# A state-space layer and an MLP in one kernel: decay rows in one load, constants regrouped, and a new head of the written order

## The chip, the cores and the metric

The kernel runs on one core of one Trainium2 chip. The core has five engines with instruction lists of their own: TensorE (PE, matmuls; PEld is its weight load), VectorE (DVE), ScalarE (ACT), GpSimd (POOL) and SyncE (SP), which here only issues transfers. Sixteen DMA engines move data between HBM and the on-chip memory. The metric is the device time of one execution in microseconds, the median of several runs.

## The reference, cut to what matters

```python
# x (4, 8, 768, 32), a (4, 8, 768), B and C (4, 8, 768, 16), all float32
log_a = np.log(np.clip(a, 1e-06, 1.0))
for c in range(nc):                       # chunks of 32 along the sequence
    cum = np.cumsum(la, axis=-1)
    L = np.exp(cum[..., :, None] - cum[..., None, :]) * causal
    M = np.einsum('bhin,bhjn->bhij', Cc, Bc) * L
    y_intra = np.einsum('bhij,bhjd->bhid', M, xc)
    y_inter = np.einsum('bhin,bhnd->bhid', Cc, state) * np.exp(cum)[..., None]
    y[:, :, sl] = y_intra + y_inter
    state = decay_full * state + sum_j(B_j x_j * decay_from_j)
x = y.transpose(0, 2, 1, 3).reshape(3072, 256)
h = x @ w_in                              # (256, 2048)
g = 0.5 * h * (1 + tanh(c * (h + 0.044715 * h**3)))
out = g @ w_out                           # (2048, 256), result (3072, 256)
```

The first half is a linear recurrence with a decay `a` per head and position, computed by chunks; the second is a two-layer MLP with the tanh form of GELU on its result.

## The kernel before, in words

The sequence of each of the 4 batches is cut into 6 chunks of 128 positions (`Q`), so there are 24 chunks, taken in 12 pairs, called units `u`. All 8 heads of a chunk are worked on together. Decays are not handled as logarithms: a reversed scan along each chunk gives the product of decays from a position to the chunk's end (`R`), B is multiplied by it, C by its reciprocal, and then the score of two positions is a plain product with a causal mask. The steps of a unit:

- `mul`, `T` or `tw`, `E` or `ew`: multiply B and C by their decays, turn them on TensorE, copy the result out of PSUM. Batch 0 has forms of its own: chunks 0 to 3 come first (`load_bc0`, `mulb`, `mulc`, `tw`, `ew`), chunks 4 and 5 later (`load_bc1`, `mul1`, `T1`, `ce1`, `bh1`). Batches 2 and 3 are turned by DMA through HBM.
- `G`: scores of a unit into four PSUM banks, `ga` (two) and `gb` (two).
- `M.u.0` and `M.u.1`: VectorE multiplies `ga` and `gb` by the causal mask (line 605). For unit 0 the second half goes another way: `GE` (line 610), ScalarE copies the two `gb` banks, and `ME` (line 616), GpSimd masks the copies.
- `XX`, `XD`, `xn`: unpack x of chunks 0 to 3 with 0/1 matrices on TensorE, and the chunks' contribution to the state; `D` is that contribution elsewhere.
- `S` and `SP`: new state, and the state scaled by the chunk's decay and spread over a block mask (lines 676 and 683, VectorE).
- `Y` and `yev`: the output of the pair, and its copy to `xm`, the input of the MLP.
- `s1.u.i` (line 709): four matmuls of the first projection into one of two `hp` banks; `gelu.u.i` (line 713) takes it to `gT`; `s2.c.q` (line 727): four matmuls of the second projection of chunk `c`; `oev` copies out, `store` writes.

The weights come as float32 in four quarters each (`load_wi`, `load_wo`), and each quarter is cast in two halves (`wi.q.k`, `wo.q.k`, line 316 on GpSimd, 314 on ScalarE, 318 on VectorE).

The decays of chunks 0 to 3 of batch 0 have a chain of their own at the start: `load_aq` (line 159, four loads of 32 rows), `clipq` (328), `Rq` (331, the scan), `tpq` (342, a transpose), `peq` (351), `recip0` (348), then `mulb`, `mulc`. `load_a` brings all decays as two halves for `clip`, `R`, `tp2`, `tp6`.

Constants are built at the start: `c_ident`, `c_tri`, `c_bmask`, `c_m8` on GpSimd, `c_cz` (a zeroed tile for C, line 254) on GpSimd, `c_wz`, `c_zero`, `c_unp` (the 0/1 matrices, lines 227 and 258 to 261), `c_sel` (271 and 273), `c_m4` (277), `c_par` on VectorE, `c_warm` (loads ScalarE's GELU table).

The order is written out by hand in `ORDERED`: one list of step names, which fixes the order of each engine's instructions. A suffix names the engine (`:A` ScalarE, `:D` VectorE, `:P` GpSimd, `:S` SyncE), `~n` is n blocks of 128 columns of filler matmuls (line 697), which compute nothing that is used, and `+4` four such blocks in front of a step. The tile framework adds the waits between engines. `deps` and `takes` are kept for the tool that made the list and do not act here.

Of the kernel before, what the change touches and what calls it, by code (L numbers as in the profile page):

```python
# [87 lines left out]
def kernel(  # L88
# [164 lines left out]
    def c_cz():  # L253
        nc.gpsimd.memset(cz, 0.0)
# [708 lines left out]
```

## Time and profile before

| | us |
|---|---|
| median of 3 runs (lowest, highest) | 116.99 (116.8, 117.34) |
| span of the profiled execution, first to last instruction | 115.1 |
| PE busy | 109.4 (95%) |
| ACT busy | 75.1 (65%) |
| DVE busy | 68.7 (60%) |
| POOL busy | 15.1 (13%) |
| share of DMA time of the 16 engines on the main queue | 53.9% |

The profile shows one execution: its instructions by engine with start and length, what an engine waited for, and the chain of work that ended last. The profiled execution itself is given by its span; the timed runs contain some 1.9 us more, which lies around the first and the last instruction. Rows of instructions read: start, length, engine, line, operation, out<-in, form, count, and in brackets the idle time before and what ended it. The granted clock is 1.00 all through on this core.

### The profile page before, as it was taken

What the parts mean: (1) busy time and instruction counts of PE and PEld (TensorE: products, weight loads), DVE (VectorE), ACT (ScalarE), POOL (GpSimd) and SP (SyncE); (2) the same over time, 40 slices, a digit from 0 to 9 for tenths busy, and PEclk for the clock granted to TensorE, in tenths of its full rate; (3) what the DMA queues carried; (4) which work ended last, traced back from release to release, by engine and by line L of the source; (5) the groups of instructions that cost most, each with busy time, mean ns of one, the idle gap of its engine ahead of it and who ended that gap; (6) DMA issues with size and microseconds to landing.
All of it is one profiled execution on the core that took longest, in us unless ns stands there. A gap on an engine that the chain in (4) does not pass through costs nothing.

```text
span 115.1 us, 3372 instructions
## 1 busy us (share of the span) xinstructions
PE 109.4 (95%) x1425; PEld 92.2 (80%) x1425; DVE 68.7 (60%) x135; ACT 75.1 (65%) x149; POOL 15.1 (13%) x32
## 2 busy tenths in 40 slices
PE   6999799999999999999999999999999999999990
PEld 2354578978877979799898998998989989999970
DVE  6688799998799989196966281546827421000100
ACT  3119889978657767657576486377766765685710
POOL 6564274122220000020002000000000000000000
PEclk9999999999999999999999999999999999999999
DMA  2999999949969828959478760000014014001132
GB/s 65 236 280 286 397 293 311 278 84 218 225 109 226 214 64 203 192 147 265 102 158 184 174 178 0 6 0 0 0 50 138 0 49 139 0 0 51 46 103 79
DMA packets 43006, 15.97 MB, mean 139 GB/s; under 512 B 36656, under 2 KB 41456, under 8 KB 42992
## 3 DMA queue, kind: packets, MB, share of 16 engines
q1 hardware_dynamic: 42848, 15.68, 53.9%
q8 instruction: 11, 0.18, 0.6%
q10 hardware_dynamic: 144, 0.08, 0.4%
q14 instruction: 3, 0.02, 0.1%
HBM read 11.04 MB, written 3.93 MB: 130 GB/s over the span
## 4 chain that ended last, share of the span: by engine, by line
PE 82%; DMA 8%; SPq 4%; POOL 1%; issue 1%; ACT 0%
PE hp L709 36%; PE o_ps L727 33%; DMA wf<-in_moe_w_out_dram 8%; PE yb L727 3%; PE ga L595 3%; PE yb L650 2%; PE yb L659 2%; SPq L190 1%; PE hp L628 1%; SPq L162 1%; SPq L159 1%; SPq L150 1%; POOL w_out_sb L316 1%; POOL w_in_sb L316 1%; SPq L183 1%
## 5 line engine op out<-in xcount | busy, mean ns | idle before, releaser
L713 ACT ACTIVATE gT<-hp 128x512 bf16<-128x512 f32 x96 | 53.3, 595 | 24.5 <-PE hp L709 24.0
L709 PE MATMUL hp<-xm,w_in_sb 128*128 128x256 bf16 x384 | 51.9, 273 | 0.5 <-ACT pend L314 0.3
L727 PE MATMUL o_ps<-w_out_sb,gT 128*128 128x256 bf16 x352 | 46.4, 273 | 0.0
L709 PEld LDWEIGHTS <-w_in_sb 128*128 128x128 bf16 x384 | 41.2, 114 | 3.2 <-issue 1.7
L727 PEld LDWEIGHTS <-gT 128*128 128x128 bf16 x384 | 37.0, 98 | 4.7 <-issue 0.8
L318 DVE COPY o_sb<-o_ps 128x256 f32<-128x256 f32 x7 | 3.0, 424 | 22.4 <-PE o_ps L727 18.4
L605 DVE TENSOR_TENSOR m<-ga,tri 128x1024 bf16<-128x1024 f32 x12 | 14.6, 1216 | 0.0
L605 DVE TENSOR_TENSOR m<-gb,tri 128x1024 bf16<-128x1024 f32 x11 | 13.4, 1219 | 0.5 <-PE gb L595 0.5
L697 PE MATMUL yb<-wz 128*128 128x512 bf16 (+2 forms) x24 | 8.2, 491 | 1.1 <-DVE warm L222 1.1
L314 ACT ACTIVATE o_sb<-o_ps 128x256 f32<-128x256 f32 x15 | 5.6, 382 | 4.1 <-PE o_ps L727 3.0
L683 DVE SCALAR_TENSOR_TENSOR sp_new<-s_new,pend,bmask 128x256 bf16<-128x256 f32 x17 | 8.0, 479 | 0.1
L316 POOL CAST x<-x_t 128x512 bf16<-128x512 f32 x5 | 3.2, 648 | 34.9 <-DMA x_t<-in_x_dram 22.9
L676 DVE SCALAR_TENSOR_TENSOR s_new<-s_new,pend,hp 128x64 f32<-128x64 f32 x13 | 3.6, 279 | 5.7 <-PE hp L628 5.5
L697 PEld LDWEIGHTS <-wz 128*128 128x128 bf16 x25 | 2.9, 126 | 5.0 <-issue 3.6
L659 PE MATMUL yb<-m,x 128*32 128x128 bf16 x192 | 6.1, 219 | 0.0
L650 PE MATMUL yb<-ce,sp_new 128*32 128x128 bf16 x160 | 5.3, 220 | 0.0
L595 PE MATMUL ga<-ce,bh 32*128 32x256 bf16 x48 | 4.7, 272 | 0.1
L314 ACT ACTIVATE xm<-yb 128x512 bf16<-128x512 f32 x8 | 4.8, 597 | 0.0
L595 PE MATMUL gb<-ce,bh 32*128 32x256 bf16 x48 | 4.7, 273 | 0.0
L727 PE MATMUL yb<-w_out_sb,gT 128*128 128x256 bf16 x32 | 4.1, 273 | 0.0
L659 PEld LDWEIGHTS <-x 128*32 128x32 bf16 x192 | 3.8, 97 | 0.4 <-issue 0.2
L650 PEld LDWEIGHTS <-sp_new 128*32 128x32 bf16 x160 | 3.0, 96 | 1.0 <-issue 1.0
(108 smaller groups left out, 78.4 us busy)
## 6 DMA issues: line engine op xcount, KB each, us to landing
out_dram<-o_sb SPq DMA_DIRECT2D x24, 128.0 KB, 2.0
x_t<-in_x_dram SPq DMA_DIRECT2D x20, 128.0 KB, 3.8
wf<-in_moe_w_in_dram SPq DMA_DIRECT2D x4, 512.0 KB, 8.3
wf<-in_moe_w_out_dram SPq DMA_DIRECT2D x4, 512.0 KB, 8.9
bc_t<-in_B_dram SPq DMA_DIRECT2D x3, 384.0 KB, 4.8
bc_t<-in_C_dram SPq DMA_DIRECT2D x3, 384.0 KB, 4.3
scr<-bc SPq DMA_DIRECT2D x4, 192.0 KB, 3.1
x_t<-in_x_dram SPq DMA_DIRECT2D x1, 512.0 KB, 4.8
```

The source lines that it names most:

```text
L314: nc.scalar.activation(o, i, AF.Copy)
L316: nc.gpsimd.tensor_copy(out=o, in_=i)
L595: nc.tensor.matmul(out=gbank(g)[:, 256 * k:256 * k + 256], lhsT=bh_of(2 * u + k)[gs], rhs=ce_of(2 * u + k)[gs], start=True, stop=True, til ...
L605: nc.vector.tensor_tensor(out=m_of(u)[:, 2 * i:2 * i + 2].rearrange("p g k e t -> p (g k e) t"), in0=gx[i].rearrange("p g (k t) -> p (g k) ...
L650: nc.tensor.matmul(out=y4[32 * j:32 * j + 32, k, w], lhsT=sp[:, 32 * h:32 * h + 32], rhs=ce_of(gc)[:, h % 2], start=first(j), stop=False, ...
L659: nc.tensor.matmul(out=y4[32 * j:32 * j + 32, k, w], lhsT=X16[u][:, k, 32 * h:32 * h + 32], rhs=m[:, h // 2, h % 2, :], start=first(j), st ...
L676: nc.vector.scalar_tensor_tensor(out=s_new, in0=state[("s", gc - 1)], scalar=pend_of(gc), in1=d, op0=ALU.mult, op1=ALU.add)
L683: nc.vector.scalar_tensor_tensor(out=sp_new.rearrange("p (g d) -> p g d", g=4), in0=(XN[0][:, H * D:H * D + 64] if gc == 0 else state[("s" ...
L697: nc.tensor.matmul(out=t[:, 0:m * 128], lhsT=wz, rhs=w3.to_broadcast([128, m, 128]), start=True, stop=True, skip_group_check=True)
L709: nc.tensor.matmul(out=hp[:, j * T:(j + 1) * T], lhsT=w_in_k[:, w, q, k], rhs=xm[:, w, u * T:(u + 1) * T], start=(w == 0), stop=(w == 1))
L713: nc.scalar.activation(gts[u][:, 2 * i:2 * i + 2], hps.pop((u, i)).rearrange("p (j t) -> p j t", j=2), AF.Gelu_apprx_tanh)
L727: nc.tensor.matmul(out=ops[gc], lhsT=gts[u][:, fi, k * Q:(k + 1) * Q], rhs=w_out_sb[:, fi, :], start=(fi == 0 and (u > 0 or k == 0)), stop ...
```

## The change

- `load_aq` becomes one load of 128 rows on SyncE, the first in its list; row 8 i + h holds positions from 32 i on of head h of batch 0. Only each fourth group of eight rows is used as a chunk. B's and C's loads follow, C first, then x of chunks 0 to 3, then weights; `load_a` goes to SyncE and stands behind two weight loads.
- `c_unp`'s zeroing becomes a step `c_unp0` on GpSimd, and its four copies one copy with a diagonal pattern. `c_cz` goes to ScalarE, as a copy of the zeroed `wz`. `c_m4`, `c_sel` and `c_unp` move behind the start of the decay chain on VectorE. `mulb` goes from GpSimd to VectorE, `mulc.1` from VectorE to GpSimd.
- `GE` and `ME` are used for units 0 and 1 instead of unit 0 alone (`GEU`), and `M.1.1` is gone.
- `SP` gets a form for GpSimd (two instructions), used for chunks 3, 6, 7 and 8.
- The list is new from its start to `castx.7` (unit 4); from there on only engine suffixes on `SP` are added. Unit 1's first projections are put between those of unit 0. The filler is 48, 4, 8 and 3 blocks instead of 53, 9, 8, 2, 13 and 4.

```diff
+GEU = (0, 1)
 ORDERED = """
-c_wz c_ident c_zero c_unp load_aq.2:A load_bc0.1 c_tri load_aq.1:S load_aq.3:S load_aq.0:A c_m8
-c_sel c_warm c_m4 load_bc0.0 load_x4 clipq Rq tpq load_a.0:A load_a.1:S peq ~53 ppq pendq:A
-load_wi.0 c_cz c_bmask recip0 mulc.0:D mulc.1:D mulb:P ~9 tw.1 tw.0 ew.0.0:D c_par ew.0.1:A tw.2
-ew.0.2:A x4.1:D ~8 G.0 clip ew.1.0:A ew.1.1:A load_wi.1 M.0.0 GE.3 x4.0:P GE.2 load_wi.2 ~2 XX.0
-XD.0 load_wo.0 xn.0:A ew.1.2:A SP.0 S.0.0 xn.1:A wi.0.0:A wi.0.1:A R ~13 G.1 S.0.1 load_wi.3 XX.1
-load_bc1.0 xn.2:A ME.3:P ME.2:P pe Y.0 XD.1 pp yev.0.0.2:A S.1.0 load_wo.1 load_bc1.1 SP.1 S.1.1
-load_wo.2 wi.1.1:P M.1.0 wi.2.0:P wo.0.0:D pend:A wo.0.1:P wi.2.1:P SP.2 wi.1.0:A M.1.1 s1.0.0
...
+c_wz load_aq c_ident c_unp0:P c_zero clipq load_bc0.1 load_bc0.0 Rq tpq c_m4 recip0 peq c_cz:A
+c_warm mulc.0:D c_sel mulb:D c_bmask c_tri c_unp mulc.1:P ~48 tw.2 tw.1 ~4 tw.0 ew.1.0:D ew.1.2:D
+ew.1.1:A ew.0.2:A ew.0.1:A load_x4 ew.0.0:A ~8 G.0 ppq M.0.0 pendq:D x4.1:P load_wi.0 load_wi.1
+load_a.1:S load_a.0:S load_wo.0 x4.0:A GE.0.2 XX.0 GE.0.3 xn.0:A xn.1:A load_wi.2 load_bc1.0
+load_bc1.1 load_wo.1 ME.0.2:P XD.0 G.1 ME.0.3:P GE.1.2 GE.1.3 S.0.0 SP.0 ~3 Y.0 XX.1 XD.1 S.0.1
+M.1.0 SP.1:D wi.1.1:D S.1.0 c_par ME.1.3:D SP.2:D clip S.1.1 wo.0.1:D wo.0.0:D R yev.0.0.2:A xn.2:A
+wi.1.0:A wi.0.1:P wi.0.0:P ME.1.2:P wi.2.1:P c_m8 wo.1.0:P s1.0.0 gelu.0.0 xn.3:A load_wi.3 s1.0.1
+gelu.0.1 load_wo.2 s1.0.2 Y.1 s1.0.3 gelu.0.2 yev.1.0.2:A gelu.0.3 load_bc.1.0 load_wo.3 load_bc.1.1
+load_x.2 s1.1.0 gelu.1.0 load_x.3 s1.1.1 gelu.1.1 wi.3.0:P wi.3.1:P wo.2.1:P wi.2.0:D tp2 recip1
+s2.0.0.0.o mul1.1 mul1.0 wo.1.1:D s1.0.4 gelu.0.4 s1.1.2 s2.0.1.0.o T1.1 gelu.1.2 s1.0.5 T1.0 s1.1.3
+s2.0.0.1.o ce1.1:A gelu.0.5 bh1:A ce1.0:D gelu.1.3 s1.1.4 G.2 s2.0.1.1.o gelu.1.4 tp6.3 tp6.2 tp6.0
+tp6.1 M.2.0 pe wo.2.0:A s1.0.6 gelu.0.6 s1.1.5 s2.0.0.2.o s1.0.7 gelu.1.5 N1 pp s2.0.1.2.o gelu.0.7
+bn1:A mul.1.0 recip.1.4 M.2.1 s1.1.6 T.1.0 wo.3.0:P wo.3.1:A pend:A E.1.0:A s2.0.0.3.o s2.0.1.3.o
+oev.1:D s1.1.7 N.1 oev.0:A gelu.1.6 gelu.1.7 SP.3:P castx.2.None:P mul.1.1 s2.1.0.0.o s2.1.0.1.o
+T.1.1 E.1.1:A bn.1:D castx.3.None:A D.2 s2.1.0.2.o S.2.0 SP.4:D s2.1.0.3.o oev.2:A Y.2 yev.2.0.2:A
...
-    def load_aq(i, eng):
-        (nc.scalar if eng == "ACT" else nc.sync).dma_start(out=aq_t[32 * i:32 * i + 32], in_=a_rows(i * Q, Q))
+    def load_aq(eng):
+        (nc.scalar if eng == "ACT" else nc.sync).dma_start(
+            out=aq_t, in_=bass.AP(tensor=a.tensor, offset=a.offset, ap=[[P4, 16], [S, H], [1, Q]]))
...
-        nc.vector.memset(unp, 0.0)
+
+    def c_unp0(eng):
+        (nc.gpsimd if eng == "POOL" else nc.vector).memset(unp, 0.0)
...
-    def c_cz():
-        nc.gpsimd.memset(cz, 0.0)
+    def c_cz(eng):
+        if eng == "POOL":
+            nc.gpsimd.memset(cz, 0.0)
+            return
+        nc.scalar.activation(cz.rearrange("p e r h n -> p (e r) (h n)"),
+                             wz.rearrange("p (o n) -> p o n", o=1).to_broadcast([128, 2 * R4, H * N]), AF.Copy)
...
-        for r in range(R4):
-            nc.vector.tensor_copy(out=unp[:, r, :, r], in_=sub)
+        d = unp[:, 0, :, 0]
+        diag = bass.AP(tensor=d.tensor, offset=d.offset, ap=[list(d.ap[0]), [Q + 1, R4], [R4, P4]])
+        nc.vector.tensor_copy(out=diag, in_=sub.rearrange("p (o q) -> p o q", o=1).to_broadcast([128, R4, P4]))
...
-    def f_GE(g):
-        nc.scalar.activation(ge0[:, g - 2], gbank(g), AF.Copy)
+    def f_GE(u, g):
+        nc.scalar.activation(ge0[GEU.index(u)][:, g - 2], gbank(g), AF.Copy)
...
+        if eng == "POOL":
+            sc = spf[gc % 2]
+            nc.gpsimd.tensor_scalar(out=sc, in0=state[("s", gc)], scalar1=pend_of(gc + 1), scalar2=None, op0=ALU.mult)
+            nc.gpsimd.tensor_tensor(out=sp_new.rearrange("p (g d) -> p g d", g=4),
+                                    in0=sc.rearrange("p (o d) -> p o d", o=1).to_broadcast([128, 4, 64]),
+                                    in1=bmask.rearrange("p (g d) -> p g d", g=4), op=ALU.mult)
+            state[("sp", gc)] = sp_new
+            return
```

More of the change, by code (lines that the diff above doesn't have):

```diff
@@ L156, in load_bc1 @@
                           .rearrange("h (p r) n -> p h (r n)", r=n))
-    def load_aq(i, eng):
-        (nc.scalar if eng == "ACT" else nc.sync).dma_start(out=aq_t[32 * i:32 * i + 32], in_=a_rows(i * Q, Q))
+    def load_aq(eng):
+        (nc.scalar if eng == "ACT" else nc.sync).dma_start(
+            out=aq_t, in_=bass.AP(tensor=a.tensor, offset=a.offset, ap=[[P4, 16], [S, H], [1, Q]]))
     def load_a(i, eng):
-        (nc.scalar if eng == "ACT" else nc.sync).dma_start(out=a_t[32 * i:32 * i + 32], in_=a_rows(i * HS, HS))
+        (nc.scalar if eng == "ACT" else nc.sync).dma_start(out=a_t[32 * i:32 * i + 32], in_=a_rows(i, HS))
     def load_bc(b, i):
@@ L297 @@
     xm = const.tile([128, 2, n_tokens], BF16, name="xm")
+    spf = [const.tile([128, 64], FP32, name=f"spf{i}") for i in range(2)]
     gx = [ps1.tile([128, 2, 512], FP32, name=f"g{i}") for i in "ab"]
@@ L752, in add @@
         return s
-    aq = [add("A", load_aq, i, alt="AS") for i in range(R4)]
+    aq = [add("S", load_aq, alt="S")]
     bl0 = {i: add("S", load_bc0, i) for i in (1, 0)}
@@ L767 @@
         wl[("o", q)].takes("wf", won[(q, 0)], won[(q, 1)])
-    ccz, cid, ctri, cbm, cm8 = (add("P", f) for f in (c_cz, c_ident, c_tri, c_bmask, c_m8))
-    add("D", c_wz)
+    cwz = add("D", c_wz)
+    ccz = add("A", c_cz, alt="AP", deps=[cwz])
+    cid, ctri, cbm, cm8 = (add("P", f) for f in (c_ident, c_tri, c_bmask, c_m8))
     cz0 = add("D", c_zero)
     add("A", c_warm, deps=[cz0])
-    cunp = add("D", c_unp, deps=[cid])
+    cu0 = add("D", c_unp0, alt="DP")
+    cunp = add("D", c_unp, deps=[cid, cu0])
     cpar = add("D", c_par, deps=[cbm])
@@ L864 @@
         Mn[u] = [add("D", f_M, u, 0, deps=[g, ctri])]
-        if u:
+        if u not in GEU:
             Mn[u].append(add("D", f_M, u, 1, deps=[g, ctri]))
```

97 lines of the change are left out of this document (45 added, 52 removed).

## The prediction

> **What bounds the kernel now.** I read the chain that ended last, then the busy time by stretch, then the timelines of the first 20 us. The chain first (shares, then pieces: start, us, what), then three stretches (us, then busy time of PE, PEld, DVE, ACT, POOL; granted clock, DMA share, GB/s):
>
> ```profile
> PE 82%; DMA 8%; SPq 4%; POOL 1%; issue 1%; ACT 0%
> 6.23 9.55 DMA wf<-in_moe_w_out_dram
> 15.83 0.87 POOL w_out_sb L316
> 14.18:18.95 4.77, 4.27 (x61) 3.38 (x60) 4.70 (x10) 4.32 (x9) 2.95 (x5) 1.00 1.01 282
> 18.95:41.84 22.89, 22.89 (x337) 19.58 (x330) 21.30 (x37) 18.06 (x36) 3.69 (x6) 1.00 0.86 191
> 41.84:112.10 70.26, 70.23 (x876) 63.31 (x876) 32.24 (x55) 45.23 (x87) 1.23 (x2) 1.00 0.37 91
> ```
>
> From 18.95 to 112.10 TensorE never stops. From 41.84 (step s1.3.3) both orders are the same list, and PE is full for 70.23 of 70.26 us. So the change is worth what it moves that moment; the tail moves with it unchanged. Ahead of it PE waits: for the decay chain to the first projection at 14.18, then for weights (the DMA piece of the chain). In 14.18 to 41.84 PE idles 0.5 us and runs four blocks of filler, 0.2 us: 0.7 us. VectorE is next, 21.30 of 22.89.
>
> The span is 115.1; the timed runs are 116.8 to 117.34, median 116.99, so 1.9 us lie around the span. I take my difference off the median.
>
> **Part 1: decay rows as one load.** SP's queue, VectorE's decay chain, and landing times:
>
> ```profile
> 0.80 0.46 SPq L150 DMA_DIRECT2D bcf<-in_C_dram  x1
> 1.32 1.03 SPq L159 DMA_DIRECT2D aq_t<-in_a_dram  x2
> 2.39 0.42 SPq L150 DMA_DIRECT2D bcf<-in_B_dram  x1
> 2.86 0.58 SPq L183 DMA_DIRECT2D x_t<-in_x_dram  x1
> 4.74 1.45 SPq L190 DMA_DIRECT2D wf<-in_moe_w_in_dram  x3
> DMA to landing us min/median/max: 2.0/2.9/3.1
> bcf<-in_C_dram SPq DMA_DIRECT2D x1, 256.0 KB, 3.1
> bcf<-in_B_dram SPq DMA_DIRECT2D x1, 256.0 KB, 3.5
> 4.10 0.17 DVE L277 TENSOR_REDUCE m<-ident 128x4 f32<-128x32 bf16 x1
> 5.16 0.23 DVE L328 TENSOR_SCALAR acq<-aq_t 128x128 f32<-128x128 f32 x1 [0.89 <-DMA aq_t<-in_a_dram]
> 6.21 0.25 DVE L351 TENSOR_SCALAR peq<-m,acq,rq_t 128x4 f32<-128x4 f32 x1
> 6.80 1.24 DVE L409 TENSOR_TENSOR cz<-bcf,pt 128x256 bf16<-128x256 f32 x2
> ```
>
> The clip waits at 5.16 for the last of four quarter loads, two of them behind C on SP. A single load goes out at 0.80. Its landing lies between 2.0 us (the earliest quarter load) and 3.1 us (the slowest): I take 2.3, nearer the load that had nothing ahead of it, a little more because it is four times the bytes. Clip at 3.15, 2.0 us earlier (bounds 1.2 to 2.3). C and B are issued at 1.3 and 1.75 and land at 4.4 and 5.25, ahead of their use. Queue times: three ACT issues go to SP's list, but the two a_t halves now stand behind two weight loads, so the first weight load is issued at about 2.9 (0.80 plus 0.5, 0.46, 0.42, 0.58) rather than 4.74. The scan of a_t is needed only at 15.
>
> **Part 2: what stands on the chain now.** Rows of the multiplies, constants and transposes:
>
> ```profile
> L409 DVE TENSOR_TENSOR cz<-bcf,pt x2: 414/659/904, 6.8 to 7.6; 128x256 bf16<-128x256 f32 x2
> 6.37 1.05 POOL L416 TENSOR_TENSOR bc0s<-bcf,rt 128x512 bf16<-128x512 f32 x1 [1.74 <-DVE rt L342]
> 1.75 0.28 DVE L258 TENSOR_REDUCE sub<-ident 128x32 bf16<-128x128 bf16 x1
> 2.41 0.94 POOL L254 MEMSET cz<- 128x1024 bf16 x1
> 2.41 1.25 DVE L271 TENSOR_REDUCE sel<-ident 128x8 f32<-128x128 bf16 x1
> 3.70 0.50 DVE L273 COPY selp<-sel 128x128 f32<-128x128 f32 x1
> 8.22 0.39 PE L425 MATMUL hp<-ident,cz 128*128 128x128 bf16 x4
> 8.92 0.38 ACT L314 ACTIVATE bh<-o_ps 128x256 bf16<-128x256 bf16 x1
> 9.08 0.28 PE L595 MATMUL ga<-ce,bh 32*128 32x256 bf16 x2
> ```
>
> From the clip to the first multiply takes 6.80 - 5.16 = 1.64, plus c_m4 0.17: multiply at 4.95. It costs 0.41 alone and 0.90 beside a GpSimd multiply; mulc.1 starts on GpSimd on the same release, so 0.85: 5.8. Then c_sel, moved onto the chain: a reduce of 0.28 (the like one at 1.75) and a copy of 0.50 at most, 0.7 with the overlap; the same reduce took 1.25 beside GpSimd's 0.94 memset, the upper end. 6.5. mulb, now on VectorE, has 512 elements: between 0.41 (256) and 0.96 (768, the row of 25.00 below), 0.69: 7.2. Transpose 0.39 as in the 8.22 row and the last copy on ScalarE 0.38: score matmul at 8.1 against 9.08, 1.0 us of the 2.0 kept. The zeroing of cz on ScalarE is 1.1 by extension from 0.38 (256) and 0.6 (512); ScalarE has nothing else until 6.7 and the use is at 4.95, so it costs nothing unless it ends over 1.5 us late. c_unp0, c_bmask and c_tri on GpSimd are needed at 8 or later. Unpacking (two instructions for five) fits behind mulb while PE transposes. The 26 blocks fewer of filler were in waits: nothing.
>
> **Part 3: score matmul to first projection (9.08 to 14.18, 5.1 us now).**
>
> ```profile
> 9.51 1.23 DVE L605 TENSOR_TENSOR m<-ga,tri 128x1024 bf16<-128x1024 f32 x1
> 9.55 1.09 ACT L610 ACTIVATE ge<-gb 128x512 bf16<-128x512 f32 x2
> 10.22 1.22 POOL L616 TENSOR_SCALAR_AFFINE_SELECT m<-ge 128x512 bf16<-128x512 bf16 x2 [1.71 <-ACT ge L610]
> 10.65 0.38 ACT L314 ACTIVATE x<-o_ps 128x256 bf16<-128x256 f32 x1
> 11.78 1.15 ACT L314 ACTIVATE w_in_sb<-wf 128x512 bf16<-128x512 f32 x2 [0.19 <-DMA wf<-in_moe_w_in_dram]
> 13.10 0.59 ACT L314 ACTIVATE xm<-yb 128x512 bf16<-128x512 f32 x1
> 13.16 0.61 POOL L316 CAST w_in_sb<-wf 128x512 bf16<-128x512 f32 x1 [1.72 <-DMA wf<-in_moe_w_in_dram]
> 14.18 1.03 PE L709 MATMUL hp<-xm,w_in_sb 128*128 128x256 bf16 x8 [0.28 <-ACT pend L314]
> ```
>
> ScalarE: GE of pair 0 at 8.6, 1.09; two x copies, 0.66: 10.35. VectorE: M.0.0 8.55 to 9.8; that frees the bank for G.1, at 9.85. ScalarE then takes the second GE pair, 1.09, to 11.5, and the y copy 0.59: 12.1. GpSimd's masks (0.62 each) and SP.0 (0.8 behind M.0.0) end by 10.6, so Y.0 is not late. Weights: the first w_in quarter was there at 11.78; its issue is 1.8 us earlier, and with queues full the lead is the earlier start of B and x plus the 96 KB moved behind, some 1.1: 10.6, then two casts of 0.61 on GpSimd: 11.9. So the first projection lies at 12.2, or 13.1 if the weights gain nothing; I take 12.45, nearer the former: 1.7 us earlier.
>
> **Part 4: 12.45 to s1.3.3.** I walked the two written lists engine by engine with these durations. On the new one, PE waits 0.3 us for the first GELU's bank, 0.5 for the y copy of pair 1 in front of s1.1.0, and in five places 0.05 to 0.1 for banks, which is 1.15 with the filler, against 0.7 now: 0.45 given back. M.1.1 (1.2 on VectorE) becomes 1.09 ScalarE, 0.62 GpSimd and 0.4 VectorE; four casts come to VectorE (0.34 each) and two copies leave it. Four SP steps go to GpSimd, 0.85 each (an estimate: 0.53 for 256 elements by the 1.05 row, 0.3 for the small multiply ahead of it); GpSimd is busy 3.69 of 22.89 us, and the last of them, SP.8, ends 1.5 us ahead of Y.4. VectorE's stalls on GpSimd:
>
> ```profile
> 16.14 0.83 DVE L683 SCALAR_TENSOR_TENSOR sp_new<-s_new,pendq,bmask 128x256 bf16<-128x256 f32 x1
> 14.00 0.48 DVE L683 SCALAR_TENSOR_TENSOR sp_new<-s_new,pendq,bmask 128x256 bf16<-128x256 f32 x1
> 25.00 0.96 DVE L475 TENSOR_TENSOR bc<-bc_t,rt 128x768 bf16<-128x768 f32 x1
> DVE bc L475 <- DMA bc_t<-in_B_dram: 0.9, 1, 0.9
> 17.88 5.74 SPq L175 DMA_DIRECT2D x_t<-in_x_dram  x2
> ```
>
> The same form takes 0.83 beside a GpSimd cast (15.83) and 0.48 without: 0.35 lost. One such on the path, half hidden, is 0.15.
> Sum: 1.7 - 0.45 - 0.15 = 1.1 us: span 114.0, median 115.9.
>
> **Rivals.**
> *GpSimd and VectorE stop each other.* In the new list VectorE has six instructions beside GpSimd's masks and casts between 11 and 18 (SP.1, wi.1.1, ME.1.3, R, wi.2.0, wo.1.1). At 0.35 each that is 2.1 us, half of it on the path: 1.05, which eats the gain: 116.9. For it: VectorE is the engine in front of Y.1. Against: GpSimd itself waits for weights between 12.6 and 15.
> [...]
>
> *Batch 1 comes too late (slower).* The new order brings mul.1.0 forward to 22.6, from 25.00, where VectorE waited for B's rows. If these and what follows land as before, it starts 2.4 late, of which 0.5 is slack; 1.9 less the 1.2 gained is 0.7 slower: 117.7. Break-even is a landing near 24. For it: SP's list blocks for 5.74 us in front of these loads. Against: one w_out quarter (1.3 us by the spacing of 11.78 and 13.16) now follows instead of leading, and all loads lead by 1.1: 22.6, just in time.
>
> *VectorE's head is blocked.* wi.1.1 waits for the second w_in quarter with S.1.0, ME.1.3 and SP.2 behind it, so s1.0.1 and Y.1 too. At 12.05 it is free; past 12.5 each us costs one. At 14.3 it costs 1.8: 117.7.
>
> *The load gains nothing* (lands 4.5 us or later): the head moves by 0.6 or less, and with 0.45 given back, 116.8.
>
> **Numbers.** Main case 0.60, 115.9 (its own range 115.0 to 116.3: the bounds of parts 1 and 3). Stops 0.10 and load 0.06, near 116.9. Batch 1 late 0.15, head blocked 0.06, both 117.7; something else slower 0.03. A measurement tells 0.5% (0.6 us) from no change. Stops could leave a little gain: faster 0.62, same 0.15, slower 0.23. Range 115.0 to 117.8.
>
> **What would show it.** Clip near 3.15 (over 4.2: part 1 wrong); first scores near 8.1 (9 and a long c_sel or mulc: part 2); s1.0.0 near 12.45 (part 3); SP and cast rows of 0.8 on VectorE: stops; VectorE waiting for bc_t or wf after 12: the slower rivals. A PE gap after 41 would break the frame.

## The result, and the profile after

The changed kernel takes 120.33 us (median of 4 runs, 120.28 to 120.64); the kernel before, on the same chip, 117.06 (116.8 to 117.34). The ratio is 1.028, with a 95% interval from 1.024 to 1.031: slower. The forecast was 115.9, so it is off by 4.4 us and on the wrong side. Single executions of a kernel can be some per cent longer than its others (e18: 119.5 to 121.79 us); such ones are left out of all ratios here and below.

First the frame of the prediction: the stretch from the first projection `s1.0.0` to `s1.3.3`, and the one from there to TensorE's last instruction. The columns are those of the prediction's stretches (us, then busy time of PE, PEld, DVE, ACT, POOL; granted clock, DMA share, GB/s). Before:

```profile
14.18:41.77 27.59, 27.09 (x390) 22.89 (x389) 25.92 (x46) 22.32 (x44) 6.64 (x10) 1.00 0.89 208
41.77:112.10 70.33, 70.30 (x883) 63.38 (x876) 32.31 (x55) 45.29 (x88) 1.23 (x2) 1.00 0.37 91
```

The same two stretches after, then 7.5 to 20 us in five pieces, and the page's line of the granted clock in 40 slices:

```profile
14.06:44.57 30.51, 30.08 (x404) 24.37 (x392) 25.89 (x54) 21.74 (x43) 12.98 (x19) 0.91 0.94 208
44.57:115.10 70.53, 70.27 (x877) 63.35 (x875) 32.43 (x54) 45.94 (x89) 1.23 (x2) 1.00 0.35 86
7.50:10.00 2.50, 1.09 (x17) 0.65 (x18) 0.97 (x3) 1.88 (x5) 0.61 (x1) 1.00 0.99 319
10.00:12.50 2.50, 1.70 (x61) 0.80 (x59) 1.59 (x5) 1.73 (x6) 2.25 (x4) 1.00 1.01 322
12.50:15.00 2.50, 2.50 (x60) 1.46 (x61) 2.50 (x8) 1.36 (x5) 0.72 (x2) 0.58 1.12 281
15.00:17.50 2.50, 2.47 (x29) 1.39 (x31) 2.50 (x8) 2.19 (x6) 2.42 (x1) 0.50 0.81 247
17.50:20.00 2.50, 2.50 (x34) 1.75 (x27) 2.36 (x9) 1.52 (x4) 1.67 (x5) 0.55 0.53 161
...
PEclk9999656999999999999999999999999999999999
```

The tail is the same to 0.2 us, so the frame holds: what counts is when `s1.3.3` starts, and it starts at 44.57 instead of 41.77. `s1.0.0` starts at 14.06, where it started at 14.18: 0.1 us of the forecast 1.7 us of lead arrived. The stretch behind it then took 2.9 us more. And from 12.9 us to just short of 20 the granted clock was half, 0.58, 0.50 and 0.55 by the last three pieces. A busy time of 2.50 in 2.50 there doesn't mean a full TensorE: 12 matmuls of the first projection took 3.09 us, and 16 of the second, of the same form, at the end of the same execution, 1.91:

```profile
14.06 3.09 PE L728 MATMUL hp<-xm,w_in_sb 128*128 128x256 bf16 x12
...
112.93 1.91 PE L746 MATMUL o_ps<-w_out_sb,gT 128*128 128x256 bf16 x16
```

Where the front lost its lead, by the timeline of the changed kernel (start, us, engine, line, operation; the bracket is the idle time before and what ended it):

```profile
3.15 0.23 DVE L339 TENSOR_SCALAR acq<-aq_t 128x128 f32<-128x128 f32 x1 [1.61 <-DMA aq_t<-in_a_dram]
5.13 0.42 DVE L420 TENSOR_TENSOR cz<-bcf,pt 128x256 bf16<-128x256 f32 x1 [0.28 <-DMA bcf<-in_C_dram]
7.33 0.42 DVE L329 COPY bh<-o_ps 128x256 bf16<-128x256 bf16 x1
7.66 0.41 DVE L329 COPY ce<-hp 128x256 bf16<-128x256 bf16 x1
8.11 0.66 ACT L325 ACTIVATE ce<-hp 128x256 bf16<-128x256 bf16 x2 [0.95 <-DVE ce L329]
8.65 0.39 ACT L325 ACTIVATE bh<-o_ps 128x256 bf16<-128x256 bf16 x1
9.10 0.28 PE L606 MATMUL ga<-ce,bh 32*128 32x256 bf16 x2 [1.41 <-ACT bh L325]
10.98 0.18 PE L584 MATMUL o_ps<-x4b,bc0s 32*32 32x64 bf16 x1 [0.63 <-ACT x L325]
14.69 0.39 ACT L325 ACTIVATE x<-hp 128x256 bf16<-128x256 f32 x1 [1.14 <-DVE s_new L687]
15.08 2.84 POOL L327 CAST w_in_sb<-wf 128x512 bf16<-128x512 f32 x1 [1.80 <-DMA wf<-in_moe_w_in_dram]
```

The clip is at 3.15, as forecast. The score matmul is at 9.10 instead of 8.1. The new list lets VectorE copy out pair 1 first (the two rows at 7.33 and 7.66); ScalarE's copies of pair 0 read the same PSUM tile and stand waiting behind VectorE's, 0.95 us by the releaser in the row at 8.11; TensorE waits 1.41 us for the last of them. In the list before, pair 0 was copied first.

### The profile page after: what moved, and what is told of

Read it like the earlier page. It is cut to its first block, busy times and chain, and to the rows that moved or that the text cites. A ratio compares the mean times of both kernels' runs of the same rounds, so it can differ in the third digit from the quotient of the medians.

```text
span 118.1 us, 3360 instructions
## 1 busy us (share of the span) xinstructions
PE 111.2 (94%) x1416; PEld 92.5 (78%) x1416; DVE 66.9 (57%) x133; ACT 76.7 (65%) x148; POOL 21.4 (18%) x40
## 4 chain that ended last, share of the span: by engine, by line
PE 79%; DVE 9%; ACT 5%; DMA 3%; issue 1%; SPq 1%; DVEq 0%
PE hp L728 35%; PE o_ps L746 30%; PE yb L746 3%; DMA bcf<-in_C_dram 3%; PE yb L661 3%; PE yb L670 3%; PE ga L606 2%; DVE m L616 2%; DVE rt L353 1%; ACT ge L621 1%; ACT gT L732 1%; DVE pt L393 1%; PE hp L639 1%; PE hp L574 1%; DVE bc L486 1%
## 5 line engine op out<-in xcount | busy, mean ns | idle before, releaser
L728 PE MATMUL hp<-xm,w_in_sb 128*128 128x256 bf16 x384 | 53.6, 280 | 0.0
L728 PEld LDWEIGHTS <-w_in_sb 128*128 128x128 bf16 x384 | 41.9, 115 | 3.8 <-issue 1.8
L616 DVE TENSOR_TENSOR m<-gb,tri 128x1024 bf16<-128x1024 f32 x10 | 12.1, 1211 | 0.3 <-PE gb L606 0.2
L716 PE MATMUL yb<-wz 128*128 128x512 bf16 (+1 forms) x16 | 6.5, 562 | 1.0 <-DVE warm L225 1.0
L327 POOL CAST x<-x_t 128x512 bf16<-128x512 f32 x4 | 2.4, 612 | 21.2 <-DMA x_t<-in_x_dram 21.2
L702 DVE SCALAR_TENSOR_TENSOR sp_new<-s_new,pend,bmask 128x256 bf16<-128x256 f32 x13 | 6.0, 477 | 0.1
L327 POOL CAST w_in_sb<-wf 128x512 bf16<-128x512 f32 x5 | 5.2, 1057 | 3.8 <-DMA wf<-in_moe_w_in_dram 3.8
L716 PEld LDWEIGHTS <-wz 128*128 128x128 bf16 x16 | 2.0, 132 | 4.0 <-issue 3.0
L325 ACT ACTIVATE xm<-yb 128x512 bf16<-128x512 f32 x7 | 4.2, 600 | 0.5 <-PE yb L670 0.4
```

The source lines that it names most:

```text
L325: nc.scalar.activation(o, i, AF.Copy)
L327: nc.gpsimd.tensor_copy(out=o, in_=i)
L616: nc.vector.tensor_tensor(out=m_of(u)[:, 2 * i:2 * i + 2].rearrange("p g k e t -> p (g k e) t"), in0=gx[i].rearrange("p g (k t) -> p (g k) ...
L702: nc.vector.scalar_tensor_tensor(out=sp_new.rearrange("p (g d) -> p g d", g=4), in0=(XN[0][:, H * D:H * D + 64] if gc == 0 else state[("s" ...
L716: nc.tensor.matmul(out=t[:, 0:m * 128], lhsT=wz, rhs=w3.to_broadcast([128, m, 128]), start=True, stop=True, skip_group_check=True)
L728: nc.tensor.matmul(out=hp[:, j * T:(j + 1) * T], lhsT=w_in_k[:, w, q, k], rhs=xm[:, w, u * T:(u + 1) * T], start=(w == 0), stop=(w == 1))
```

## The experiments

All edits are in `ORDERED`, but for e7, which takes a part of the change over into the kernel before. Some change one thing; e8, e9, e12 and e16 to e18 change several at once. The ratio is that to the kernel before on the same chip; the columns behind it are those of the profiled execution.

| run | median us | ratio (95%) | s1.0.0 at | s1.3.3 at | clock |
|---|---|---|---|---|---|
| kernel before | 117.0 to 117.6 | 1 | 14.18 | 41.77 | 1.00 |
| changed kernel | 120.33 | 1.028 (1.024 to 1.031) | 14.06 | 44.57 | 0.971 |
| e1_fill_both | 119.38 | 1.015 (1.008 to 1.023) | 13.62 | 44.38 | 0.984 |
| e2_fill_second | 119.62 | 1.017 (1.008 to 1.025) | 13.73 | 44.06 | 1.000 |
| e3_fill_first | 119.35 | 1.016 (1.008 to 1.023) | 13.52 | 43.84 | 0.996 |
| e4_before_less_fill | 118.46 | 1.002 (0.997 to 1.008) | 15.07 | 44.40 | 0.971 |
| e5_unp_later | 119.09 | 1.015 (1.009 to 1.022) | 13.59 | 43.31 | 1.000 |
| e6_s1_early | 119.52 | 1.019 (1.013 to 1.026) | 13.66 | 43.80 | 1.000 |
| e7_load_alone | 117.52 | 0.999 (0.994 to 1.003) | 14.04 | 42.44 | 0.985 |
| e8_pair0_first | 118.73 | 1.013 (1.005 to 1.022) | 12.82 | 42.93 | 0.995 |
| e9_front_new_back_old | 122.54 | 1.038 (1.026 to 1.050) | 12.73 | 47.15 | 0.972 |
| e10_sp_on_vector | 118.77 | 1.007 (1.002 to 1.012) | 12.43 | 42.95 | 1.000 |
| e11_loads_of_before | 120.44 | 1.024 (1.017 to 1.030) | 13.54 | 44.86 | 0.999 |
| e12_front_new_loads_old | 123.29 | 1.041 (1.028 to 1.053) | 13.60 | 48.25 | 0.970 |
| e13_no_scalar_waits | 118.81 | 1.012 (1.005 to 1.020) | 12.68 | 42.90 | 1.000 |
| e14_pe_and_wo3_early | 119.53 | 1.018 (1.009 to 1.028) | 12.56 | 43.33 | 1.000 |
| e15_back_mend_alone | 119.90 | 1.021 (1.012 to 1.029) | 13.74 | 44.79 | 1.000 |
| e16_hybrid_mended | 118.82 | 1.014 (1.009 to 1.019) | 12.69 | 42.78 | 0.998 |
| e17_both_gaps | 120.12 | 1.012 (1.006 to 1.018) | 12.88 | 44.52 | 0.986 |
| e18_scan_early | 120.11 | 1.022 (1.016 to 1.027) | 12.63 | 44.33 | 0.986 |

Medians of two rows can come from different chips, and the executions of some kernels lie 2.4 to 3.5 us apart (e4, e7, e10, e17), so the ratio, not the median, is what compares. None is shown to be faster than the kernel before.

### The clock: filler put back, filler taken away

```diff
e1, after:   -ew.0.0:A ~8 G.0          +ew.0.0:A ~32 G.0
             -ME.0.2:P XD.0            +ME.0.2:P ~14 XD.0
e2: only the ~14      e3: only the ~32
e4, before:  -R ~13 G.1                +R G.1
             -~2 XX.0                  +XX.0
```

> The changed kernel with 24 filler blocks more ahead of the first score matmuls (TensorE idled 1.41 us there) and 14 more ahead of XD.0 (it idled 0.63 and 0.28 us there); nothing else. Theory A (the empty stretches let the clock fall to 0.50 from 12.9 to 19.9 us, and the half rate is the loss): the granted clock stays 1.00 and the time falls by most of half of the 7.0 us, to 116.5 to 117.5. Theory B (late data and waits hold the start, the clock is beside it): the clock may stay up, but the time stays within 0.5 of 120.3.

> The changed kernel with only the 14 filler blocks ahead of XD.0 (10.35 to 11.26 us). [...] Theory A with any idle microsecond: the gap of 1.41 us ahead still drops the clock, time about 120. Theory B: 120.3.

> The changed kernel with only the 24 filler blocks ahead of the first score matmuls (7.7 to 9.1 us). [...] Theory A with any idle microsecond as the cause: partly helped. Theory B: 120.3.

> The kernel before without its 13 filler blocks ahead of G.1 and the 2 ahead of XX.0; nothing else. Theory A: the granted clock falls near 12 to 13 us for some 7 us as in the changed kernel, and the time rises by 2 to 3.5 us to 119 to 120.5. Theory B: the filler fills waits only, the time stays within 0.3 of 117.0.

The changed kernel's four executions had a mean granted clock of 0.969 to 0.971. Of the twelve of e1 to e3 two were below 0.99 (0.984 in e1, 0.967 in e2), so either filler alone kept the clock at 0.99 or more in 7 of 8. That the later gap alone decides is refuted by e3, where only the earlier gap is filled and the clock was 0.996 or more in all four. The filler is worth 0.7 to 1.0 us by the medians (120.33 to 119.35, 119.38 and 119.62) and 1.3 to 1.4 by the ratios, which take the chip out. It isn't the whole loss, though theory A put it there (116.5 to 117.5): e2, at full clock, is still 1.7% slower than before. What comes instead of the slow clock is seen in e2, by the stretch from `s1.0.0` to `s1.3.3` and TensorE's waits (us in total, times, longest):

```profile
13.73:44.06 30.33, 27.82 (x406) 23.50 (x391) 27.17 (x55) 21.49 (x43) 12.64 (x19) 1.00 0.89 211
...
PE ga L606 <- ACT bh L325: 1.4, 1, 1.4
...
PE hp L728 <- ACT x L325: 0.9, 1, 0.9
PE hp L404 <- DVE pe L398: 0.6, 1, 0.6
PE hp L728 <- ACT gT L732: 0.4, 1, 0.4
PE hp L728 <- ACT xm L325: 0.4, 1, 0.4
```

At full clock the stretch is as long as at half clock (30.33 against 30.51), now with 2.51 us idle instead of 0.43. By the granted clock of the three pieces from 12.5 to 20 us the slow clock took 1.05, 1.25 and 1.13, 3.4 us of TensorE's work; little of it was lost, by the equal length of the stretch, since a faster TensorE would have waited, as in e2.

The reverse, e4, shows the same drop without the change (0.72, 0.50 and 0.50 in the three pieces from 12.5 to 20 us). Its line of granted clock:

```profile
PEclk9999855999999999999999999999999999999999
```

Its ten executions fall in groups by the clock: 117.09 us at 1.00 (one), 117.25, 117.25, 117.56 and 118.89 at 0.985, 118.4 to 119.46 at 0.971 (five). By the span of 117.7 us I estimate a mean of 0.985 as some 3.5 us at half clock, one of 0.971 as some 6.8. So the shorter drop costs 0.2 to 0.5 us here, but for one execution, and the longer one 1.3 to 2.4, against a single execution at full clock. That is mostly less than the 2 to 3.5 expected. Whether an execution meets the drop varies, and the filler makes it rare: nine of ten are below 0.99 here, two of thirteen of the kernel before on the same chip.

In the changed kernel the clock fell behind gaps of 1.41 and 0.63 us, with TensorE busy 1.09 and 1.70 us in the two pieces of 2.50 that hold them.

### The score matmul: what holds it at 9.1

```diff
e5, on e1 with ~20 for ~32:
-c_unp mulc.1:P ~48 ... ew.1.0:D ew.1.2:D
+mulc.1:P ~48 ... ew.1.0:D ew.1.2:D c_unp
e8, on the changed kernel:
-ew.1.0:D ew.1.2:D ew.1.1:A ew.0.2:A ew.0.1:A load_x4 ew.0.0:A ~8 G.0
+ew.0.2:A ew.0.1:A ew.0.0:D ew.1.1:A ew.1.2:D load_x4 ew.1.0:A ~12 G.0
-ME.0.2:P XD.0                 +ME.0.2:P ~14 XD.0
-M.1.0 SP.1:D wi.1.1:D S.1.0   +M.1.0 S.1.0 SP.1:D wi.1.1:D
```

> The changed kernel with filler in both gaps (12 and 14 blocks more), and with VectorE's build of the unpack matrix (0.36 + 0.31 us, 6.72 to 7.49) moved behind its two casts for pair 1 (ew.1.0, ew.1.2). Theory W (ScalarE's cast ew.0.2 starts only when VectorE's read of the same transposed tile is over, so what VectorE does first sets G.0): ew.0.2 starts at 7.4 instead of 8.11, G.0 at 8.4 instead of 9.1, and the time falls by 0.4 to 0.7 from the 119.4 of the kernel with filler in both gaps. Rival (batch 0's x, landing at 8.2 and cast at 8.9, or the weights, hold the start): G.0 earlier, time the same within 0.3.

> The changed kernel with filler in the gaps, pair 0's three casts ahead of pair 1's (two on ScalarE, one on VectorE, which share no tile), and S.1.0 ahead of SP.1 and the weight cast. Theory W: G.0 near 7.9 instead of 9.1, x cast at 8.2, masks 0.7 us earlier, s1.0.0 near 13.0 and the second step near 13.8; time 117.6 to 118.4. Rival (half of the loss lies in the order behind 14 us: weights late, ScalarE and VectorE full): time above 118.6.

I had thought that the unpack constants (the copy at 7.18 on VectorE) held pair 1's copy. That is refuted. In e5 they stand behind it, and VectorE waits idle all the same:

```profile
7.30 0.42 DVE L329 COPY bh<-o_ps 128x256 bf16<-128x256 bf16 x1 [0.65 <-PE o_ps L436]
...
8.10 0.66 ACT L325 ACTIVATE ce<-hp 128x256 bf16<-128x256 bf16 x2 [0.85 <-DVE ce L329]
```

VectorE's first copy needs the last transpose, the second stands behind it in the list, and ScalarE waits for the second. With pair 0 first, in e8:

```profile
8.06 0.28 PE L605 MATMUL ga<-ce,bh 32*128 32x256 bf16 x2
...
12.82 0.62 PE L727 MATMUL hp<-xm,w_in_sb 128*128 128x256 bf16 x4
...
12.82:42.93 30.11, 28.18 (x407) 23.58 (x391) 26.40 (x55) 21.48 (x43) 12.16 (x19) 1.00 0.86 207
```

The scores start at 8.06, where the prediction had put them, and `s1.0.0` at 12.82, 1.36 us ahead of the kernel before. Ahead of the scores e8 differs in the order of these copies, in one of pair 0's going from ScalarE to VectorE, and in four blocks of filler; the order, which sets what waits for what, was thus what kept parts 2 and 3 from coming true. That 8.06 meets the forecast 8.1 so well is partly luck, as two terms of part 2 were off in opposite directions (below). But `s1.3.3` is still 1.2 us later than before: by the table the stretch takes 29.7 to 31.1 us in e1 to e3, e5, e6, e10 and e13 to e15 too, whether the front of the new order is late, early or at half clock.

### One load alone, in the order of before

```diff
-c_wz c_ident c_zero c_unp load_aq.2:A load_bc0.1 c_tri load_aq.1:S load_aq.3:S load_aq.0:A c_m8
+c_wz load_aq c_ident c_zero c_unp0:D c_unp load_bc0.1 c_tri c_m8
```

> The order of the kernel before, with one part of the change alone: the decay rows as one load, first on SyncE, ahead of C and B, and the unpack matrix filled by one copy. Theory of the prediction (the decay chain sets the first score matmuls, and what it gains is kept): the first score matmuls 0.8 to 1.0 us earlier than 9.08, time 116.0 to 116.6. Rival (batch 0's x, cast behind its load, which is 0.5 later now, or the weights hold the rest): score matmuls earlier, time 117.0 within 0.3 or up to 0.5 slower.

Its score matmul starts at 8.45, 0.63 us earlier, but `s1.0.0` at 14.04, only 0.14 earlier, and the time is the same (0.999, from 0.994 to 1.003). ScalarE shows what stands between:

```profile
11.64 1.15 ACT L324 ACTIVATE w_in_sb<-wf 128x512 bf16<-128x512 f32 x2 [0.68 <-DMA wf<-in_moe_w_in_dram]
12.70 0.36 ACT L324 ACTIVATE x<-hp 128x256 bf16<-128x256 f32 x1
```

ScalarE waits for the first weights, and the x copy of the head stands behind the two casts. So the load alone shortens the decay chain, and the weights, cast ahead of that copy, take the gain back.

### The stretch behind s1.0.0: one piece at a time

```diff
e6, on e1:   -SP.1:D wi.1.1:D S.1.0        +S.1.0 SP.1:D wi.1.1:D
e10, on e8:  -SP.3:P SP.7:P SP.6:P SP.8:P  +SP.3:D SP.7:D SP.6:D SP.8:D
e13, on e8:  -M.1.0 S.1.0 SP.1:D wi.1.1:D ... S.1.1 ... wi.1.0:A wi.0.1:P wi.0.0:P
             +SP.1:D S.1.0 S.1.1 wi.1.1:D M.1.0 ... wi.0.1:P wi.0.0:P wi.1.0:P
e14, on e13: pe ahead of s1.0.4 instead of behind M.2.0; load_wo.3 ahead of load_bc.1.0
e15, on e1:  the edit of e13
```

> The changed kernel with filler in both gaps, and with VectorE's S.1.0 put ahead of SP.1 and of a weight cast (0.48 + 0.42 us). Theory W (xn.2 on ScalarE waits for S.1.0's read of the same PSUM tile, and the second up-projection step waits for xn.2): xn.2 starts near 14.0 instead of 14.7 to 14.8, the second step 0.7 us earlier, the time lower by 0.3 to 0.7 than 119.4. Rival (weights and ScalarE's queue hold the steps behind it): time the same within 0.3.

> The kernel with pair 0's casts first and S.1.0 early (118.73), with SP.3, SP.6, SP.7 and SP.8 back on VectorE (0.48 us each) from GpSimd (0.45 + 0.67 us each). Theory G (GpSimd's two steps, and what they stop on VectorE, cost the stretch behind 25 us): time 0.3 to 0.8 lower. Rival (they are hidden, as the waits of TensorE do not name them): same within 0.3, or up to 0.5 slower, since VectorE is full from 22 to 41 us.

> The kernel with pair 0's casts first (118.73), with S.1.0 and S.1.1 ahead of M.1.0 on VectorE and one weight cast (wi.1.0, 0.62 us) from ScalarE to GpSimd, so that ScalarE's xn.2, xn.3 and GELUs come without waits. Theory B (the waits of the first four up-projection steps, 1.95 us of TensorE between 13.2 and 17.3, are part of the loss): they shrink to 0.8 or less and the time falls by 0.6 to 1.1, to 117.6 to 118.1. Rival (later work, the weights or pair 1's x, holds the next steps, and the gap only moves): s1.1.0 and the time the same within 0.3.

> As the kernel without ScalarE's waits, and also pe (VectorE) ahead of its transposes, and the load of wo.3 ahead of bc.1.0, against TensorE's gaps at 24.5 to 27 us. Theory B: the gaps there fall from 0.8 to 0.2 and the time by 0.3 to 0.6 more, to 117.1 to 117.7. Rival (VectorE, full from 22 to 35 us, holds the stretch): same as the kernel without ScalarE's waits within 0.3.

> The changed kernel with filler in both gaps (119.38) and only the mend of the first four up-projection steps (S.1.0 and S.1.1 ahead of M.1.0, wi.1.0 on GpSimd), without pair 0's casts first. Theory B: the mend is worth 0.6 to 1.1 here too, time 118.3 to 118.8. Rival: the same within 0.3.

None of the five shows a gain clear of noise. In e6 the copy is half a microsecond earlier and TensorE waits for `gT` (0.6), the y copy (0.4) and the next x copy (0.4) instead. e10 doesn't show that SP on GpSimd cost anything: `s1.3.3` comes at 42.95 against 42.93 and the medians are alike (118.77 and 118.73), though a step on GpSimd took 1.12 us (0.45 and 0.67) and not 0.85. By the ratios e10 is 0.6% lower, with intervals that overlap, so the point isn't settled. In e13 a row of small waits is left (0.4 for the x copy, 0.3 for B's multiply of batch 0, several of 0.2); in e15 TensorE's longest wait behind `s1.0.0` is 0.9 us, at 38.79, for VectorE's mask of unit 3. Shortening the waits of the first steps thus didn't shorten the stretch, as the rivals had it. e14 is a miss: `s1.3.3` is 0.4 us later, not earlier.

### Old order behind the new front, old loads with the new list

```diff
e9, on e8: from s1.0.0 on the list of before, with wo.1.0:P still ahead of s1.0.0
e12:       e9 with the load order of before, clip and R early on VectorE, and c_m8, pe and pp earlier
e11:       e8 with the load order of before (a, then w_in 0 to 2, w_out 0, ...)
e16:       e9 with wo.1.0:P in its old place, e13's order ahead of s1.0.0,
           and weights in the order wi.0 wi.1 wo.0 wi.2 wi.3
```

> The kernel with pair 0's casts first and S.1.0 early as far as the first up-projection step (its loads too), and from there the order of the kernel before (its few steps that stood ahead of that point, pe, pp and pend among them, put where their data is there). Theory O (the loss lies in the new order behind the first up-projection: from s1.0.0 to s1.3.3 it takes 30.1 us, the order of before took 27.6): the stretch falls to 28.0 or less, s1.3.3 near 41.0, time 115.5 to 116.6. Rival (the late weights of the front, wi.3 near 20 and w_out behind it, hold whatever order follows): the stretch stays above 29, time 117.5 or more.

> As the kernel with the new front and the old order behind it, and also the loads in the order of before, and VectorE's clip and scan of the other batches' decay rows (0.35 + 0.94 us) put back into its idle stretch near 10 us. Theory O: the stretch from s1.0.0 to s1.3.3 is 27.6 to 28.2 and s1.3.3 comes at 40.6 to 41.4: time 115.4 to 116.4, faster than before. Rival (something of the new front holds the rest): the stretch above 28.5, time 117 or more.

> The kernel with pair 0's casts first and S.1.0 early (118.73), with its loads behind x issued in the order of the kernel before (the rows of a first, all of w_in early, then w_out). Theory L (the new order of loads, which brings wi.3 at 20.2 instead of 17.0 and bc1 early, costs it): time 0.5 to 1.2 lower. Rival (the order of the engines' own queues holds: ScalarE's casts between the GELUs and the late scan): same within 0.4.

> The new front (one decay load, pair 0's casts first, S.1.0 and S.1.1 early, wi.1.0 on GpSimd; s1.0.0 near 12.7), its weights loaded as wi.0, wi.1, wo.0, wi.2, wi.3, and behind s1.0.0 the order of the kernel before, with wo.1.0 in its old place on GpSimd. Theory O (the new order behind the first up-projection is the loss): the stretch from s1.0.0 to s1.3.3 takes 27.6 to 28.4 instead of 30.2, s1.3.3 comes at 40.3 to 41.2, and the time is 115.6 to 116.4, below the kernel before. Rival (what the front takes from VectorE, GpSimd and the loads is missing behind it in any order: the weights and the casts of 13 to 20 us hold): the stretch above 28.8, the time 117.0 or more.

e9 and e12 don't answer the question: GpSimd's cast of a late w_out quarter stood ahead of the w_in casts, and TensorE waited 3.3 and 3.0 us for these. e11 does: with the old order of loads the first projection waits 0.8 us for its weights, `s1.3.3` comes 1.9 us later than in e8, and the run is slower by 1.7 us by the medians and 1.0% by the ratios. So theory L is refuted: the new order of loads is the better one for the new list.

e16 splits the stretch. Its stretches, its rows of 11 to 20 us, and one row of the kernel before (`s1.0.6`):

```profile
12.69:18.00 5.31, 2.90 (x39) 2.14 (x22) 5.21 (x13) 3.22 (x7) 2.28 (x5) 1.00 0.98 301
18.00:42.78 24.78, 24.78 (x372) 21.11 (x370) 22.91 (x43) 19.24 (x39) 4.58 (x7) 1.00 0.83 189
...
11.07 1.72 POOL L326 CAST w_in_sb<-wf 128x512 bf16<-128x512 f32 x3
11.73 1.92 DVE L701 SCALAR_TENSOR_TENSOR sp_new<-s_new,pendq,bmask 128x256 bf16<-128x256 f32 x1
12.74 0.63 POOL L626 TENSOR_SCALAR_AFFINE_SELECT m<-ge 128x512 bf16<-128x512 bf16 x1
13.88 0.38 ACT L324 ACTIVATE x<-hp 128x256 bf16<-128x256 f32 x1 [1.25 <-DVE s_new L686]
14.31 0.60 PE L727 MATMUL hp<-xm,w_in_sb 128*128 128x256 bf16 x4 [1.00 <-ACT x L324]
16.14 0.47 DVE L701 SCALAR_TENSOR_TENSOR sp_new<-s_new,pendq,bmask 128x256 bf16<-128x256 f32 x1
17.61 0.61 PE L745 MATMUL o_ps<-w_out_sb,gT 128*128 128x256 bf16 x4 [1.41 <-DVE w_out_sb L328]
19.91 1.12 PE L727 MATMUL hp<-xm,w_in_sb 128*128 128x256 bf16 x8
...
18.95 1.06 PE L709 MATMUL hp<-xm,w_in_sb 128*128 128x256 bf16 x8
```

From 18 us on the old order runs TensorE without a pause, with two gaps ahead of that, 2.4 us together. The first is in part VectorE beside GpSimd: the same instruction takes 1.92 us at 11.73, beside GpSimd's casts and mask, which end at 13.37, and 0.47 at 16.14, where GpSimd is idle; the new state and the x copy stand behind it. The second is the cast of w_out, late in VectorE's list behind the same things. So the 1.5 us of lead at `s1.0.0` is more than gone: `s1.0.6` comes at 19.91, 1.0 us behind the kernel before. From there to `s1.3.3` both take the same, 22.9 and 22.8 us.

Last, both gaps attacked, in two ways:

```diff
e17, on e16: -SP.1:D S.1.0 S.1.1 wi.1.1:D M.1.0 c_par   +S.1.0 S.1.1 wi.1.1:D wo.0.0:D M.1.0 SP.1:D c_par
             wo.0.1 from VectorE to GpSimd; four blocks of filler ahead of s1.0.4 and s1.0.6
e18:         e17 with clip and R ahead of S.1.0, and pp behind s1.0.7
```

> The mended hybrid (118.82) with S.1.0 and S.1.1 ahead of SP.1 on VectorE, and the two casts of wo.0 ahead of M.1.0 (VectorE) and ahead of wi.2's (GpSimd); 8 filler blocks ahead of s1.0.4 and s1.0.6, where weights may be late. Theory: the two gaps (1.16 and 1.58) were all that the front's gain was lost to; without them only wi.2 (landed at 14.7 there) and wi.3 (17.5) hold s1.0.4 and s1.0.6, which come at 16.0 and 18.2 (18.95 in the kernel before); s1.3.3 at 40.7 to 41.2, time 116.0 to 116.7, faster than before by 0.3 to 1.0. Rival (the gap only moves on to the next late piece): s1.3.3 above 41.8, time 117 or more.

> The last hybrid with VectorE's clip and scan of the other batches' rows in its idle stretch at 12 us, pe right behind SP.2, and pp behind s1.0.7. Theory (the lead is real, and each loss so far was one late piece in a queue): s1.0.6 near 18.0 to 18.3 (18.95 in the kernel before), no gap over 0.5 behind it, s1.3.3 at 40.6 to 41.2 (41.77 before), time 116.0 to 116.6 at full clock. Rival (the pieces are late because VectorE, GpSimd and the loads have no room between 12 and 20 us for an earlier start): another gap of a microsecond, s1.3.3 above 41.7, time 117 or more.

In e17 the first gap is 0.37 us instead of 1.00, so the long SP was worth 0.6 of it, and the second is gone. TensorE was through with `Y.1` at 17.85, 1.1 us ahead of the kernel before, and then stopped for the decay transposes, whose input is the scan that now came late. The profile is of an execution at a clock of 0.986 (120.17 us); two of the six ran at full clock, 118.13 and 118.79 us, which is still 1.2% slower than before, and whether they stop there as long isn't shown; e18 moves the scan forward into the time of GpSimd's casts. One row of e17, then four of e18:

```profile
19.55 0.37 PE L403 MATMUL hp<-pe,selp 64*128 64x24 f32 x2 [1.70 <-DVE pe L397]
```

```profile
12.19 1.34 DVE L338 TENSOR_SCALAR ac<-a_t 64x384 f32<-64x384 f32 x1 [0.54 <-DMA a_t<-in_a_dram]
13.56 1.24 DVE L341 TENSOR_TENSOR_SCAN r_t<-ac,ends 64x384 f32<-64x384 f32 x1
14.73 0.24 DVE L686 SCALAR_TENSOR_TENSOR s_new<-s_new,pendq,hp 128x64 f32<-128x64 f32 x1
15.44 0.60 PE L727 MATMUL hp<-xm,w_in_sb 128*128 128x256 bf16 x4 [2.18 <-ACT x L324]
```

The clip takes 1.34 us beside casts and a mask of GpSimd (0.34 in e16 with GpSimd idle) and the scan 1.24 (0.94 in the kernel before, with GpSimd idle); TensorE waits 2.18 us, and the clock goes down behind the longest gap of both: 0.75 and 0.57 in 15 to 20 us here, 0.68 and 0.64 in 20 to 25 us of e17 (mean 0.986 in both). Each mend of one place opened another.

## Why the prediction was wrong

**The frame** held: 0.2 us of the 3.0 us of difference lies behind `s1.3.3`.

**Part 1** held: clip at 3.15. C landed at 5.0 and not 4.4, its first multiply starting at 5.13 instead of 4.95; by itself that is 0.2 us. The queue's times were put too short as well: the first weight load went out at 3.78, not about 2.9. But e7 shows what I had only as a rival of 0.06: without a new list the gain doesn't pass the weights.

**Part 2** failed at its last step, "transpose 0.39 as in the 8.22 row and the last copy on ScalarE 0.38: score matmul at 8.1". I costed the last copy and not the queue that it stands in: ScalarE's copies of pair 0 share a PSUM tile with VectorE's copy of pair 1, which the new list puts first. TensorE waits 1.41 us for it, 1.0 of which shows in the sum; e8 gives that back (8.06). The rest was hidden by another error: the first C multiply on VectorE took 0.42 and not 0.85 (GpSimd's beside it took 0.87), so the chain to the end of `mulb` was 0.4 us shorter than forecast. In e8 B's rows held `mulb` back by 0.25, and small waits around the copies used up the rest. `cz` on ScalarE (1.06, forecast 1.1) and `mulb` (0.69) were priced right. The terms of this part as written add up to 8.0, not 8.1.

Its sentence "the 26 blocks fewer of filler were in waits: nothing" failed as well. They were in waits, and filler in such waits kept the clock (0.99 or more in ten of the twelve executions of e1 to e3, 0.969 to 0.971 in the changed kernel): 0.7 to 1.0 us by the medians of e1 to e3 and 1.3 to 1.4 by their ratios, on a kernel with long gaps in its front.

**Part 3** was right once its start was right: from 8.1 to 12.45 forecast, from 8.06 to 12.82 measured in e8, so 0.4 was missing.

**Part 4** is the step that decided the sign: "which is 1.15 with the filler, against 0.7 now: 0.45 given back", and 0.15 for stops, so a stretch of some 28.2 us. It took 30.3 at full clock (e2), 30.1 with the front mended (e8). The waits in it, 0.95 forecast, measured 2.51 in e2 and 1.93 in e8. Of e2's 2.7 us over before, 2.0 is idle time of TensorE (2.51 against 0.50), 0.4 (its busy time in e8) the decay transposes `pp` (line 404 in e2), which were ahead of the stretch before and are in it now and which I didn't count, and 0.3 isn't assigned by the rows (0.7 in e8), or more, as the stretch before also held a little filler. My walk of the lists gave each instruction its duration alone and each queue its work, and missed chains across queues: the x copy behind the new state, behind SP, behind a cast. That this one chain isn't the whole of it is seen in e6, e13 and e15, which mend it without shortening the stretch; which chain sets its length stays open.

The sum in the profiled executions: forecast span 114.0, measured 118.1. By e2, at full clock, `s1.0.0` is 1.3 late against 12.45 and the stretch 2.1 long; the tail is 0.2, and the rest, 0.5, is put down to the clock (117.6 against 118.1), though two single executions differ by as much at the same clock (e10: 118.04 and 118.98 us, both at 1.00).

**The rivals.** *GpSimd and VectorE stop each other*: in the changed kernel it is hardly VectorE that takes longer: of the six instructions named, `wi.2.0` took 0.76 instead of 0.42 and the others their usual time. GpSimd does, one cast of 0.58 taking 2.84, which no TensorE wait names. In e16 and e18, where the front is early, VectorE does, by 1.45 and 1.0 us and not by 0.35. So the rival's price was three to four times too low for these; on the path it is 0.6 us in e16, by the first gap there and in e17. The rows show that these instructions lie beside GpSimd's casts and masks; why they take longer there isn't shown.

*Batch 1 too late*: no, VectorE's waits after the change don't list B's rows at all. *VectorE's head is blocked*: not as I put it; `wi.1.1` at 14.05 waited for no weights, it follows SP.1 without idle time. *The load gains nothing*: not by a late landing, but by its effect, in the old order.

What stays open: whether some order keeps the lead of 1.4 us that the new front can have. The edits of the places behind it didn't find one. That the resources forbid it isn't shown. What makes the unassigned part of the stretch's excess, and why the stretch is as long at half clock as at full clock to 0.2 us, I haven't settled either; the second may be chance. That ScalarE's wait comes from the shared PSUM tile is read from the releaser in its rows and from e8, where the order of the copies is turned; two tiles instead of one weren't tried.

## What to carry to other kernels

In a list scheduled by hand, a step's price is its duration plus what its queue is doing: for each copy that ends a chain, look who else reads or writes the same PSUM tile, on which engine, and what that engine waits for just ahead (here 0.95 us behind VectorE's copy). A lead at one point is worth only what the next late input leaves of it (in e7 0.14 of 0.63 us); before counting it, look for what ends last behind that point, here weights, casts and a chain through VectorE. And filler in waits isn't free to remove: here TensorE was idle for 2.2 us of 5, the granted clock was half for some 7 us behind that, and the profile showed TensorE as busy there, 2.47 to 2.50 us of each 2.50.

## What the runs showed of the hardware

- In the changed kernel the granted clock fell from 1.00 to 0.50 at 12.9 us, behind 5 us (7.5 to 12.5) in which TensorE was busy 2.8 and no gap was over 1.41. It stayed at half for about 7 us there; about 3.5 is the estimate for the profiled execution of e1 (0.54 and 0.78 in the two pieces from 15 to 20 us, mean 0.984). With filler in one of the two gaps, either one, the mean stayed at 0.99 or more in 7 of 8 executions.
- Some instructions of VectorE and GpSimd took longer beside each other: on VectorE 1.92 us instead of 0.47 (e16) and 1.34 instead of 0.34 (e18), on GpSimd 2.84 instead of 0.58 (changed kernel), beside a VectorE that was busy 2.50 of 2.50 us in both pieces from 12.5 to 17.5.
